# Block differences of w_out one place sooner each on VectorE, and one add ahead of the maxima of batch 3

## Chip, cores and metric

The kernel runs on one core of a Trainium2 chip. The metric is device time in microseconds (us), the median of three runs. The engines are TensorE (PE, with PEld for its weight loads), VectorE (DVE), ScalarE (ACT), GpSimd (POOL) and SyncE (SP, which here only issues transfers).

## What is computed

For each of 8 batches and 8 heads, 512 rows `x` and 32 rows `state` of width 64 read one another by attention (scale 1/8, softmax), and the result of 544 rows by 512 columns per batch goes through two dense layers with a leaky ReLU between them:

```
scores  = scale * x @ state^T          xread = softmax(scores)  @ state     # 512 rows
scores2 = scale * state @ x^T          sread = softmax(scores2) @ x         # 32 rows
x = concat([xread, sread], rows), heads side by side                        # (8*544) x 512
h = x @ w_in ; g = max(0.01*h, h)      # w_in 512 x 2048
out = g @ w_out                        # w_out 2048 x 512, fp32 out
```

## The kernel before

**Per batch.** `a_scores` puts both score matrices of a batch into one PSUM tile `sc`. The first softmax is taken over blocks of 32: `a_max` (L266), `a_diff` (a spread by 32x32 transposes, L274, and a subtraction, L280), `a_exp` (ACT, L284), `a_recip` (L289 sum, L293, L296, L298 spread), `a_probs` (L302, tile `aT`). The second softmax goes along rows: `a_max2` (L331, "the second maxima", tile `mcol`), `a_exp2` (ACT, L337, once for each half g), `a_probs2` (L345, L347, two of L355). `a_m` multiplies the states into w_in (L407, tile `M`, evicted by L421 or L1113), so that the first layer `ff1` is 16 steps s of two 512-column matmuls (L428) with a leaky ReLU on ACT (L433, tile `hT`). `a_sread` (L380) makes the 32 state rows. While batch b runs its 16 steps, the softmax of batch b+1 (`nxt`) is done between the steps.

**The second layer.** Batch 0 and half of batch 1 multiply `hT` by w_out directly (`piece`, L456; `y_store`, L466, copies a finished row block out and stores it). The rest uses a 2x2 block scheme with seven block products instead of eight: w_out is cut into blocks of 1024 rows by 256 columns, and four differences of these blocks are made once, by `tw_sum` (L495), in bf16, each in two halves of 128x1024 on DVE or four quarters of 128x512 on POOL:

- `tw[1]`: block (0,1) minus block (0,0), on POOL
- `tw[2]`: block (1,1) minus `tw[1]`, on DVE
- `tw[3]`: block (1,1) minus block (0,1), on DVE
- `tw[4]`: block (1,0) minus `tw[2]`, on DVE

Their consumers are the products: n=5 takes `tw[1]`, n=6 `tw[2]`, n=7 `tw[3]`, n=4 `tw[4]` (`w_of`). The other half of batch 1 is `two_product` (L602), done between the steps of batch 2 in the order n = 1, 2, 6, 5, 3, 7, 4 at s = 2, 3, 5, 6, 8, 9, 11. Its hT-side sums are `two_sum` (L586, tiles `Sr`); products 1, 6 and 5 are copied to `rkept` by ACT (L607), products 2, 7 and 3 are added to a kept one by DVE (L612, tile `ysb`), product 4 is copied by ACT (L609). Below these are called product 1, product 2 and so on, and the three adds of L612 add 2, add 3 and add 7. From batch 2 on `product` and `s_sum` (L551, L516) do the same for whole batches.

**Order.** The order of the instructions on each engine is written out by hand: the program's order is the order of each engine's queue, and each engine takes its own in order. At batch 2 the order at the two steps that the change touches is:

```
s == 1: a_scores(nxt) ... a_max(nxt) ... a_diff(nxt); a_max2(nxt); two_sum(q1, 3, 0, 8, nc.vector)
s == 3: two_product(q1, 2)                       # with add 2 on DVE
s == 4: a_exp(nxt) ...; tw_sum(4, ...) on DVE
```

**Other places that the steps touch.** Before batch 1, the x rows of batch 1 are cast in two halves on DVE (L898), transposed on PE (L918, tile `pxt`) and copied (L921). `state_cast` (L209) scales a group of states: for batches 2 and 3 on DVE, for batches 4 to 7 on POOL at batch 2's s = 8 (tile `stb`), after which SP issues the transposes `st_t` (L214) and, for batch 4, `xT` (L234). `cast_all` (L132) is POOL's cast of a whole batch of x, loaded by SP (L99, tile `xl`) into `xb`.

Of the kernel before, what the change touches and what calls it, by code (L numbers as in the profile page):

```python
# [27 lines left out]
def kernel(  # L28
# [9 lines left out]
    nc = tc.nc  # L38
# [290 lines left out]
    def a_max2(a):  # L329
        a.m2 = att.tile([P, 2], FP32, name="mcol", tag="mcol")  # L330
        nc.vector.tensor_reduce(out=a.m2[:], in_=a.sc[:], axis=AX.X, op=ALU.max, negate=True)  # L331
# [118 lines left out]
    def piece(b, hT, i, jq, bank=None, copy=SCA, js=range(4)):  # L450
        if jq == 0 and js[0] == 0:
            y = ys[b, i] = Y()
            y.py = psum.tile([P, DM], FP32, name="py", tag="py")[:] if bank is None else bank
        y = ys[b, i]
        for j in [4 * jq + v for v in js]:
            nc.tensor.matmul(  # L456
                y.py, lhsT=hT[:, j, P * i:P * (i + 1)], rhs=w_out_bf[:, j, :],
                start=(j == 0), stop=(j == 15),
            )
        if jq == 3 and copy is not None:  # L460
            y_store(b, i, copy)
# [8 lines left out]
    HJ = 8  # L470
# [12 lines left out]
    def w_block(r, c, j0, j1):  # L483
        return w_out_bf[:, HJ * r + j0:HJ * r + j1, HN * c:HN * (c + 1)]

    def tw_sum(n, j0, j1, eng):
        u, at = j0 // 4, slice(j0 % 4, j0 % 4 + j1 - j0)
        in0, in1 = {
            1: lambda: (w_block(0, 1, j0, j1), w_block(0, 0, j0, j1)),
            2: lambda: (w_block(1, 1, j0, j1), tw[1][u][:, at]),  # L490
            3: lambda: (w_block(1, 1, j0, j1), w_block(0, 1, j0, j1)),
            4: lambda: (w_block(1, 0, j0, j1), tw[2][u][:, at]),
        }[n]()
        with nc.allow_low_precision(reason="operands of bf16 products"):
            eng.tensor_tensor(out=tw[n][u][:, at], in0=in0, in1=in1, op=ALU.subtract)  # L495
# [431 lines left out]
    a_shift(a1)  # L927
    a_max2(a1)
    tw_open()
    for j in range(0, HJ, 2):  # L930
        tw_sum(1, j, j + 2, nc.gpsimd)
    for i in (0, 1):
        piece(0, h0, i, 1)
# [21 lines left out]
    for v in range(2):  # L955
        for i in (2, 3):
            piece(0, h0, i, 3, copy=None, js=range(2 * v, 2 * v + 2))
    for i in (2, 3):
        y_store(0, i, VEC)
    cast_all(3)  # L960
# [6 lines left out]
    for s in range(16):  # L967
        ff1(a1, h1, s)
        if s % 2:
            pb, hT, i, jq = fill[s // 2]  # L970
            piece(pb, hT, i, jq)
        if s in (1, 15):
            for u in range(2):
                tw_sum(2 if s == 1 else 3, 4 * u, 4 * (u + 1), nc.vector)
        if s == 3:
            a_scores(a2)
            m_evict(a2, 0, a_m(a2, 0, "big"), SCA)
            a_shift(a2)
            a_max2(a2)
        elif s == 7:  # L980
            a_exp(a2)
            a_open(att_of[3], 3)
            a_xt_dma(att_of[3])
        elif s in (9, 11):
            a_exp2(a2, s // 2 - 4)
            if s == 9:
                a_recip(a2)
                a_probs(a2)
            else:
                a_probs2(a2)  # L990
        elif s == 13:
            a_probs2(a1)
            a_a2t_pair(0)
            pm = [a_m(a2, 1, "big"), a_m(a2, 2, "sc")]
            m_evict(a2, 1, pm[0], VEC)
            m_evict(a2, 2, pm[1], SCA)
# [3 lines left out]
    for b in range(2, B):  # L1000
        hT = hpool.tile([P, 16, S], BF16, name="hT", tag="hT")
        hTs[b] = hT
        a = att_of[b]
        nxt = att_of[b + 1] if b + 1 < B else None
        if b == 2:
            q1 = two_open(h1, 2 * P, ("S0", "S1"), "py")
            two_keep(q1, "S2")
            fill = {i: [lambda i=i: piece(1, h1, i, 3)] for i in range(2)}
            for s, n in zip((2, 3, 5, 6, 8, 9, 11), (1, 2, 6, 5, 3, 7, 4)):
                fill[s] = [lambda n=n: two_product(q1, n)]  # L1010
            fill[11].append(lambda: nc.sync.dma_start(pair_rows(1, 1), q1.y[:]))
        else:
            order = (2, 6, 5, 7, 3, 4)
            fill = {
                s: [lambda n=order[s // 2], v=s % 2: product(b - 1, n, v)] for s in range(12)
            }
            for i, n in enumerate(order):
                if n not in (2, 7):
                    fill[2 * i + 1].append(lambda n=n: after(b - 1, n))
        fill[12 if b < 6 else 13] = [lambda: product(b, 1, 0)]  # L1020
        fill[14] = [lambda: product(b, 1, 1, 0, 4)]
        fill[15] = [lambda: product(b, 1, 1, 4, 8), lambda: after(b, 1)]
        for s in range(16):
            ff1(a, hT, s)
            if s == 0:
                if b == 2:
                    load_x(4, nc.sync)
                if b + 2 < B:
                    open_xb(b + 2)
                if b == 7:  # L1030
                    a_a2t_pair(6)
                elif b != 6:
                    a_a2t(a)
                for n in (1, 2):
                    if b > 2:
                        s_sum(b - 1, n, 4, 8, nc.vector)
                    else:
                        two_sum(q1, n, 0, 8, nc.vector)
            elif s == 1:
                if nxt is not None:  # L1040
                    a_scores(nxt)
                m_evict(a, 3, a_m(a, 3, "big"), SCA)
                if nxt is not None:
                    a_max(nxt)
                if b > 2:
                    for j in range(0, HJ, 2):
                        s_sum(b - 1, 4, j, j + 2, nc.gpsimd)
                else:
                    for j in (0, 4):
                        two_sum(q1, 4, j, j + 4, nc.gpsimd)  # L1050
                if b + 2 < B:
                    cast_all(b + 2)
            elif s == 4:
                if b == 2:
                    load_state(1)
                    a_sread(a0)
            elif s == 7:
                if b == 2:
                    a_sread(a1)
            elif s == 13:  # L1060
                if b < 6:
                    a_sread(a)
            elif s == 8:
                if b == 2:
                    state_cast(1, nc.gpsimd)
                    state_t(1)
            elif s == 10:
                if b == 7:
                    a_sread(att_of[6])
            elif s == 12:  # L1070
                if b == 7:
                    a_sread(a)
                for n in (1, 2):
                    s_sum(b, n, 0, 4, nc.vector)
                for j in (0, 4):
                    s_sum(b, 3, j, j + 4, nc.vector)
            if nxt is not None:
                if s == 4:
                    a_exp(nxt)
                elif s in (6, 7):  # L1080
                    a_exp2(nxt, s - 6)
                    if s == 7:
                        a_recip(nxt)
            if b == 2 and s == 4:
                for u in range(2):
                    tw_sum(4, 4 * u, 4 * (u + 1), nc.vector)
            if s == 9 and b + 2 < B:
                a_open(att_of[b + 2], b + 2)
                a_xt_dma(att_of[b + 2])
                if b + 3 < B:  # L1090
                    load_x(b + 3, nc.sync)
            for f in fill.get(s, ()):
                f()
            if s == 1:
                if b > 2:
                    after(b - 1, 2)
                if nxt is not None:
                    a_diff(nxt)
                    a_max2(nxt)
                if b == 2:  # L1100
                    two_sum(q1, 3, 0, 8, nc.vector)
            elif s == (8 if b == 2 else 7):
                if b > 2:
                    after(b - 1, 7)
                if nxt is not None:
                    a_probs(nxt)
                    a_probs2(nxt)
            elif s == 10 and nxt is not None:
                pm2 = a_m(nxt, 2, "phpy")
                pm0 = a_m(nxt, 0, "big")  # L1110
                pm1 = a_m(nxt, 1, "sc")
                for g, copy in enumerate((SCA, VEC)):
                    copy(nxt.M[:, g, 2 * DM:3 * DM], pm2[g][:])  # L1113
                m_evict(nxt, 0, pm0, VEC)
                m_evict(nxt, 1, pm1, SCA)
# [4 lines left out]
    b = B - 1  # L1120
# [21 lines left out]
    for n in (1, 2, 6, 5, 7, 3, 4):  # L1142
        two_product(q, n)
        if n in (3, 4):
            u = n - 3
# [43 lines left out]
```

## Time and profile before

| what | us |
|---|---|
| median of 3 runs | 206.49 (206.26 to 206.52) |
| profiled execution, its own time | 206.81 |
| its span (first to last instruction) | 205.0 |
| PE busy in the span | 198.6 (97%) |
| DVE busy | 150.9 (74%) |
| ACT busy | 142.2 (69%) |
| POOL busy | 62.3 (30%) |

The granted TensorE clock is 1.0. In the rows below the first number is the start in us from the span's beginning, the second the time until the last of the row's instructions ended; "x2" is two of them in a row; the bracket at the end is the idle time of the engine before the row and what ended it. Differences between starts are used where instructions overlap their neighbour's end, as matmuls do.

### The profile page before, as it was taken

What the parts mean: (1) busy time and instruction counts of PE and PEld (TensorE: products, weight loads), DVE (VectorE), ACT (ScalarE), POOL (GpSimd) and SP (SyncE); (2) the same over time, 40 slices, a digit from 0 to 9 for tenths busy, and PEclk for the clock granted to TensorE, in tenths of its full rate; (3) what the DMA queues carried; (4) which work ended last, traced back from release to release, by engine and by line L of the source; (5) the groups of instructions that cost most, each with busy time, mean ns of one, the idle gap of its engine ahead of it and who ended that gap; (6) DMA issues with size and microseconds to landing.
All of it is one profiled execution on the core that took longest, in us unless ns stands there. A gap on an engine that the chain in (4) does not pass through costs nothing.

```text
span 205.0 us, 4489 instructions
## 1 busy us (share of the span) xinstructions
PE 198.6 (97%) x1832; PEld 129.9 (63%) x1832; DVE 150.9 (74%) x222; ACT 142.2 (69%) x274; POOL 62.3 (30%) x67
## 2 busy tenths in 40 slices
PE   7999999999999899999999999999999999999993
PEld 2743444344465567766776677676767677788882
DVE  2765897799999999979997998699879402823512
ACT  3579767688989687867787779686958655846220
POOL 8914640030244076006700580054005400540000
PEclk9999999999999999999999999999999999999999
DMA  5999999685693796945093505220026202210115
GB/s 188 220 207 298 255 259 143 162 289 102 136 302 76 95 224 192 218 173 157 4 258 152 155 3 104 104 105 0 0 105 166 39 3 102 102 54 0 56 36 169
DMA packets 38741, 27.75 MB, mean 135 GB/s; under 512 B 24384, under 2 KB 35776, under 8 KB 38720
## 3 DMA queue, kind: packets, MB, share of 16 engines
q1 hardware_dynamic: 33552, 20.78, 39.2%
q0 software_dynamic: 4832, 6.29, 15.0%
q10 hardware_dynamic: 336, 0.39, 0.8%
q8 instruction: 14, 0.23, 0.5%
q14 instruction: 7, 0.06, 0.1%
HBM read 17.30 MB, written 8.91 MB: 128 GB/s over the span
## 4 chain that ended last, share of the span: by engine, by line
PE 71%; DVE 13%; DMA 8%; POOL 3%; issue 1%; ACT 1%; ACTq 1%; POOLq 0%
PE ph L428 19%; PE ppx L551 17%; PE ppb L551 15%; DMA x<-in_x_dram 7%; PE ppr L602 3%; PE ph L439 3%; PE pyw L456 3%; PE py L456 3%; PE ppw L551 3%; PE pm L407 3%; DVE tw L495 2%; POOL w_in_bf L145 2%; PE psr L380 1%; DVE sh L274 1%; PE sc L256 1%
## 5 line engine op out<-in xcount | busy, mean ns | idle before, releaser
L433 ACT ACTIVATE hT<-ph 128x512 bf16<-128x512 f32 x112 | 66.3, 602 | 26.6 <-PE ph L428 25.7
L428 PE MATMUL ph<-aT,M 128*128 128x512 bf16 x224 | 65.3, 379 | 0.0
L516 POOL TENSOR_TENSOR S<-hT,S 128x512 bf16<-128x512 bf16 x24 | 31.7, 1340 | 78.6 <-DVE S L516 61.5
L551 PEld LDWEIGHTS <-S 128*128 128x128 bf16 x384 | 37.6, 98 | 12.9
L551 PEld LDWEIGHTS <-hT 128*128 128x128 bf16 x288 | 27.7, 98 | 11.9 <-issue 1.9
L516 DVE TENSOR_TENSOR S<-hT 128x1024 bf16<-128x1024 bf16 x24 | 25.4, 1082 | 4.4 <-ACT hT L433 4.4
L428 PEld LDWEIGHTS <-M 128*128 128x128 bf16 x224 | 20.8, 98 | 9.3 <-issue 3.6
L551 PE MATMUL ppx<-tw,S 128*128 128x256 bf16 x160 | 20.7, 273 | 0.0
L456 PEld LDWEIGHTS <-hT 128*128 128x128 bf16 x96 | 9.0, 97 | 11.5 <-issue 1.3
L456 PE MATMUL py<-w_out_bf,hT 128*128 128x512 bf16 x64 | 16.0, 379 | 0.0
L132 POOL CAST xb<-xl 128x2048 bf16<-128x2048 f32 x5 | 9.5, 1895 | 18.1 <-DMA xl<-in_x_dram 15.2
L642 DVE TENSOR_TENSOR ysb<-ppb,s 128x512 f32<-128x512 f32 x12 | 8.3, 688 | 7.6 <-PE ppb L551 7.6
L421 ACT CAST M<-pm 128x1024 bf16<-128x1024 f32 x13 | 13.2, 1014 | 0.6 <-PE pm L407 0.6
L551 PE MATMUL ppb<-w_out_bf,hT 128*128 128x256 bf16 x96 | 12.5, 273 | 0.0
L551 PE MATMUL ppb<-tw,S 128*128 128x256 bf16 x96 | 12.4, 273 | 0.0
L551 PE MATMUL ppb<-w_out_bf,S 128*128 128x256 bf16 x96 | 12.3, 273 | 0.0
L551 PE MATMUL ppx<-w_out_bf,hT 128*128 128x256 bf16 x80 | 11.2, 273 | 0.0
L337 ACT ACTIVATE e<-sc,mcol 128x512 bf16<-128x512 f32 x16 | 11.1, 696 | 0.0
L289 DVE TRANSPOSE_TENSOR_REDUCE r<-e 128x32 f32<-128x1024 bf16 x7 | 8.7, 1243 | 2.4 <-ACT e L284 2.4
L551 PE MATMUL ppx<-tw,hT 128*128 128x256 bf16 x80 | 10.4, 273 | 0.0
L331 DVE TENSOR_REDUCE mcol<-sc 128x2 f32<-128x1024 f32 x8 | 9.7, 1215 | 0.0
L443 ACT ACTIVATE hs<-ph 128x256 bf16<-128x256 f32 x16 | 6.0, 387 | 5.0 <-PE ph L439 4.6
(135 smaller groups left out, 304.3 us busy)
## 6 DMA issues: line engine op xcount, KB each, us to landing
out_dram<-ysb SPq DMA_DIRECT2D x11, 512.0 KB, 2.7
xl<-in_x_dram SPq DMA_DIRECT2D x5, 1024.0 KB, 6.7
out_dram<-ysb SPq DMA_DIRECT2D x9, 256.0 KB, 5.1
w_in_bf<-in_moe_w_in_dram POOLq DMA_DIRECT2D x4, 512.0 KB, 9.2
xf<-in_x_dram SPq DMA_DIRECT2D x4, 256.0 KB, 3.9
w_out_bf<-in_moe_w_out_dram POOLq DMA_DIRECT2D x4, 256.0 KB, 13.8
x<-in_x_dram POOLq DMA_DIRECT2D x2, 512.0 KB, 14.2
w_out_bf<-in_moe_w_out_dram POOLq DMA_DIRECT2D x2, 512.0 KB, 15.5
```

The costliest lines, as they stand in the source:

```text
L132: nc.gpsimd.tensor_copy(xt[b][:].rearrange("p t h d -> p h t d"), xl[b][:].rearrange("p h (t d) -> p h t d", t=NT),)
L289: nc.vector.tensor_reduce(out=r1[:], in_=e1[:].rearrange("p (c j) -> p c j", j=NS), axis=AX.X, op=ALU.add, apply_transpose=True,)
L331: nc.vector.tensor_reduce(out=a.m2[:], in_=a.sc[:], axis=AX.X, op=ALU.max, negate=True)
L337: nc.scalar.activation(out=a.e2[:, g], in_=a.sc[:, g, :], func=AF.Exp, bias=a.m2[:, g:g + 1], accum_out=a.r2[:, g:g + 1],)
L407: nc.tensor.matmul(at[v][NS * r:NS * (r + 1)], lhsT=st_of(a, g, k), rhs=w_in_bf[D * g:D * (g + 1), k, DM * c:DM * (c + 1)], start=True, st ...
L421: copy(a.M[:, :, cols], pm[:])
L428: nc.tensor.matmul(ph[:], lhsT=a.M[:, g, P * j:P * (j + 1)], rhs=a.aT[:, g, :], start=(g == 0), stop=(g == 1),)
L433: nc.scalar.activation(out=hT[:, j, :], in_=ph[:], func=AF.Prelu, scale=1 / SCALE, alpha=0.01)
L456: nc.tensor.matmul(y.py, lhsT=hT[:, j, P * i:P * (i + 1)], rhs=w_out_bf[:, j, :], start=(j == 0), stop=(j == 15),)
L516: eng.tensor_tensor(out=part(n), in0=in0, in1=in1, op=op)
L551: nc.tensor.matmul(q[bank][v], lhsT=lhsT, rhs=w_of(n, j), start=q["open", bank] and j == 0, stop=j == 7, skip_group_check=True,)
L642: nc.vector.tensor_tensor(out=to, in0=of, in1=in1, op=ALU.add)
```

## The change

The reorder of POOL's four quarters of `tw[1]` puts blocks 4 to 7 ahead of blocks 0 to 3. Each DVE pair of `tw_sum` moves one place up: `tw[2]` from batch 1's s = 1 to behind the last pieces of batch 0, `tw[3]` from batch 1's s = 15 to its s = 1, `tw[4]` from batch 2's s = 4 to batch 1's s = 15. At batch 2, the second maxima and the third `two_sum` move from s = 1 to s = 3, behind `two_product(q1, 2)` and so behind add 2. No instruction is added or removed; the order on PE, ACT and SP stays as it was.

```diff
@@ before batch 1 @@
-    for j in range(0, HJ, 2):
+    for j in (4, 6, 0, 2):
         tw_sum(1, j, j + 2, nc.gpsimd)
...
             piece(0, h0, i, 3, copy=None, js=range(2 * v, 2 * v + 2))
+    for j in (0, 4):
+        tw_sum(2, j, j + 4, nc.vector)
     for i in (2, 3):
         y_store(0, i, VEC)
@@ batch 1 @@
         if s in (1, 15):
             for u in range(2):
-                tw_sum(2 if s == 1 else 3, 4 * u, 4 * (u + 1), nc.vector)
+                tw_sum(3 if s == 1 else 4, 4 * u, 4 * (u + 1), nc.vector)
@@ batches 2 to 7 @@
-            if b == 2 and s == 4:
-                for u in range(2):
-                    tw_sum(4, 4 * u, 4 * (u + 1), nc.vector)
...
                 if nxt is not None:
                     a_diff(nxt)
-                    a_max2(nxt)
-                if b == 2:
-                    two_sum(q1, 3, 0, 8, nc.vector)
+                    if b > 2:
+                        a_max2(nxt)
+            elif s == 3 and b == 2:
+                a_max2(nxt)
+                two_sum(q1, 3, 0, 8, nc.vector)
```

## The prediction

> **What bounds the kernel now.** I read the page's chain of waits first, then TensorE's (PE's) timeline around every place where the chain leaves PE, then the timelines of the engines that it goes to.
>
> ```profile
> PE 71%; DVE 13%; DMA 8%; POOL 3%; issue 1%; ACT 1%; ACTq 1%; POOLq 0%
> ```
>
> The end is set by PE, except for 13% of the span on VectorE (DVE). So a change on DVE is worth what PE's gaps in that part are worth, and no more. PE's timeline shows the gaps (start, time, engine, line; in brackets idle time and its releaser):
>
> ```profile
> 23.03 0.61 PE L918 MATMUL pxt<-ident,xb 128*128 128x128 bf16 x8
> 23.88 0.62 PE L918 MATMUL pxt<-ident,xb 128*128 128x128 bf16 x8 [0.24 <-DVE stf L902]
> 24.34 0.59 PE L456 MATMUL pyw<-w_out_bf,hT 128*128 128x512 bf16 x2
> ...
> 57.04 1.04 PE L602 MATMUL ppr<-w_out_bf,hT 128*128 128x256 bf16 x8
> ...
> 60.12 0.59 PE L428 MATMUL ph<-aT,M 128*128 128x512 bf16 x2
> 60.85 1.05 PE L602 MATMUL ppr<-tw,Sr 128*128 128x256 bf16 x8
> ...
> 62.63 0.59 PE L428 MATMUL ph<-aT,M 128*128 128x512 bf16 x2
> 63.06 1.04 PE L602 MATMUL ppr<-w_out_bf,Sr 128*128 128x256 bf16 x8
> ...
> 65.24 0.59 PE L428 MATMUL ph<-aT,M 128*128 128x512 bf16 x2
> 65.77 0.39 PE L407 MATMUL pm<-w_in_bf,st_t 64*32 64x512 bf16 x1
> 66.75 0.84 PE L407 MATMUL pm<-w_in_bf,st_t 64*32 64x512 bf16 x23 [0.60 <-DVE ysb L612]
> 67.53 0.60 PE L428 MATMUL ph<-aT,M 128*128 128x512 bf16 x2
> 68.61 1.03 PE L602 MATMUL ppr<-tw,hT 128*128 128x256 bf16 x8 [0.48 <-DVE ysb L612]
> ```
>
> By starts: a transpose group takes 0.46 (23.88 to 24.34), but the first one held PE 0.85, a gap of 0.39. A pair of L428 takes 0.43 (62.63 to 63.06), so product 5 at 60.85 is 0.30 late, the matmuls for M are about 0.95 late (65.77 to 66.75 for one of them), and product 4 at 68.61 is 0.65 late. Together 2.29 us: the most that this change can return. DVE ends all of these waits; its rows:
>
> ```profile
> 21.28 0.68 DVE L898 CAST xb<-x 128x1024 bf16<-128x1024 f32 x1
> 22.22 1.60 DVE L898 CAST xb<-x 128x1024 bf16<-128x1024 f32 x1 [0.26 <-DMA x<-in_x_dram]
> ...
> 36.86 1.29 DVE L466 COPY ysb<-pyw 128x512 f32<-128x512 f32 x2 [1.31 <-PE pyw L456]
> ...
> 40.69 1.25 DVE L266 TRANSPOSE_TENSOR_REDUCE mrow<-sc 128x32 f32<-128x1024 f32 x1 [0.41 <-PE sc L256]
> ...
> 52.42 1.29 DVE L495 TENSOR_TENSOR tw<-w_out_bf 128x1024 bf16<-128x1024 bf16 x2
> ...
> 58.65 1.22 DVE L331 TENSOR_REDUCE mcol<-sc 128x2 f32<-128x1024 f32 x1
> 59.78 0.68 DVE L586 TENSOR_TENSOR Sr<-hT 128x1024 bf16<-128x1024 bf16 x1
> 60.38 0.42 DVE L612 TENSOR_TENSOR ysb<-ppr,rkept 128x256 f32<-128x256 f32 x1
> 60.71 2.04 DVE L495 TENSOR_TENSOR tw<-w_out_bf,tw 128x1024 bf16<-128x1024 bf16 x1
> ...
> 63.28 1.23 DVE L289 TRANSPOSE_TENSOR_REDUCE r<-e 128x32 f32<-128x1024 bf16 x1
> ...
> 65.15 1.25 DVE L298 STREAM_TRANSPOSE qb<-qh 128x1024 bf16<-128x1024 bf16 x1
> 66.32 0.39 DVE L612 TENSOR_TENSOR ysb<-ppr,rkept 128x256 f32<-128x256 f32 x1
> 66.63 0.67 DVE L302 TENSOR_TENSOR aT<-e,qb 128x1024 bf16<-128x1024 bf16 x1
> ...
> 67.61 0.62 DVE L355 TENSOR_SCALAR a<-e,qc 128x512 bf16<-128x512 bf16 x2
> 68.14 0.42 DVE L612 TENSOR_TENSOR ysb<-ppr,rkept 128x256 f32<-128x256 f32 x1
> ```
>
> From 40.69 on DVE is full. Two of its rows are far too long: the second L898 cast (1.60 beside 0.68) and the first tw difference at 60.71 (2.04, where the pair at 52.42 took 1.29 together). GpSimd's (POOL's) rows lie across both:
>
> ```profile
> 22.12 2.71 POOL L495 TENSOR_TENSOR tw<-w_out_bf 128x512 bf16<-128x512 bf16 x2 [0.78 <-DVE xb L898]
> 25.90 2.27 POOL L495 TENSOR_TENSOR tw<-w_out_bf 128x512 bf16<-128x512 bf16 x2 [1.06 <-DMA w_out_bf<-in_moe_w_out_dram]
> ...
> 60.31 1.90 POOL L132 CAST xb<-xl 128x2048 bf16<-128x2048 f32 x1 [2.86 <-PE ppr L602]
> 65.08 1.50 POOL L209 TENSOR_SCALAR stb<-stf 128x512 bf16<-128x512 f32 x1 [2.87 <-DMA stf<-in_state_dram]
> ```
>
> So while POOL works, some DVE instructions stand: the difference issued at 60.71 ended at 62.75, 0.54 behind POOL's 62.21, and with 0.68 of its own it began about 62.07, 0.14 before POOL's recorded end.
>
> **POOL's order.** The quarters of blocks 4 to 7 wait for w_out until 25.90 in either order, and now stand first. Nothing of POOL lies on the cast at 22.22 any more: it ends at 22.90 instead of 23.82, the second transposes follow the first at 23.49, and PE is 0.39 earlier from there. POOL ends at about 30.4 (25.90 + 4 x 1.13) instead of 28.17. The first reader of tw[1] is DVE's new place at 35.16 (36.86 - 1.31 - 0.39), so 4.7 us of other work cover that; past them, a delay would hold DVE's queue us for us.
>
> **tw[2] behind batch 0.** DVE idles 1.31 ahead of 36.86, waiting for PE's pieces. The pair costs 1.29 and fills this hole; were it later, the copies, batch 0's second probabilities and tw[3] stand behind it, and only the 0.41 idle before 40.69 absorbs it. I price it at nothing. tw[3] takes tw[2]'s place and tw[4] takes the place at 52.42, pair for pair. So everything from 40.69 to 58.65 moves by the 0.39 that PE gained, and no more.
>
> **Batch 2.** What stood on DVE from 58.65 was maxima, Sr 3, add 2, two tw differences, L289. Now it is add 2, maxima, Sr 3, L289. The steps from start to start are 0.33 (60.38 to 60.71), 1.13 (58.65 to 59.78) and 0.60 (59.78 to 60.38). Add 2 starts at 58.65 - 0.39 = 58.26; product 2 ended at 57.04 + 1.04 = 58.08, now 57.69, so it waits for nothing. Maxima 58.59, Sr 3 59.72, L289 60.32: 2.96 before 63.28, of which 0.39 is the early gain and 2.57 the tw pair with its stall. ScalarE (ACT) doesn't forbid it:
>
> ```profile
> 59.58 1.06 ACT L284 ACTIVATE e<-sh 128x1024 bf16<-128x1024 f32 x1
> ...
> 64.53 1.07 ACT L433 ACTIVATE hT<-ph 128x512 bf16<-128x512 f32 x2
> ```
>
> L289's input was there at 60.64, now 60.25. With add 2 gone by 58.7, product 5 loses its 0.30.
>
> What is late next: POOL's cast asks for its turn at 60.31 - 0.39 = 59.92, if its transfer moves with the rest: SP issues it behind the transposes of batch 0's second probabilities, which DVE writes. Sr 3 was first by 0.20, so POOL waits about 0.35 and DVE nothing. Then L298 at 62.19 (+1.87), add 3 at 63.36, held to about 63.45 by product 3 (63.06 + 1.04 less 0.69), L302 at 63.76, L355 at 64.74. POOL's state cast, whose transfers follow in the same queue, moves to 64.69 and holds until 66.19 - 0.14 = 66.05. L355 falls inside. Its kind (one input, no PSUM) was not seen beside POOL; it costs between nothing and a stall to 66.05. I take the stall, by the nearest row: the L898 cast has one input too and was held. Then add 7 starts at 66.05 + 0.53 = 66.58 and product 4 at 67.05 (+0.47, as 68.14 to 68.61): 1.56 earlier than 68.61.
>
> The Trainium skill, SBUF — State Buffer, section "Who interferes with whom", says that a DVE instruction with two SBUF inputs, or a copy, cast or tensor_scalar in a two-port mode, takes a port pair that POOL needs too, for the whole instruction, and that whichever starts first keeps the other out. That rule speaks against this change, since it moves a two-input sum to within 0.2 us of a POOL cast; by it the sum would be rival 2's where POOL is first, and by the rows alone 1.56.
>
> Behind product 4 PE has no gap of this size until batch 3, where the transposed x of batch 4 could be late:
>
> ```profile
> 67.90 3.03 SPq L234 DMA_TRANSPOSE xT<-xb  x1
> ...
> xT<-xb SPq DMA_TRANSPOSE x1, 5.4
> ...
> 75.25 0.41 PE L256 MATMUL sc<-xT,st_t 64*32 64x512 bf16 x8
> ```
>
> It landed at 73.30; its issue follows POOL's state cast, so now 72.9, and PE asks at 75.25 - 1.56 = 73.69. That holds. The sum is **-1.56 us**: 0.39 early and 1.17 at batch 2. Against the profiled execution's own 206.81 that is 205.25; the median of the runs is 0.32 lower, 206.49, and gives 204.9.
>
> **Rivals.** (1) The state cast comes later than L355's second half, or doesn't hold it. Then add 7 starts at 65.27 and PE is the later one. ACT's queue of activations was back to back until 65.60, so PE's pair at 65.24 gains only about 0.44 (to 64.80); the next pair follows 2.29 - 0.95 = 1.34 later, product 4 0.43 after it, 66.57: -2.04, 204.4. For it: the two are 0.05 us apart. Against it: the cast lasts 1.50 and need only touch the second half.
>
> (2) POOL's cast at 59.92 gets in ahead of Sr 3. Sr 3 starts at 61.81 - 0.14 = 61.67, L289 at 62.27, add 3 at 65.31, and L302 at 65.62 meets the state cast, until 66.05. Product 4 then starts 1.98 later (66.63 to 68.61), 68.03: -0.58, 205.9. Without the second meeting it is 67.60: -1.01, 205.5. For it: a lead of 0.20 against a transfer. Against it: both follow from the same DVE work.
>
> (3) Rival 2, and no early gain, because PE's second transposes wait for something other than the cast (the row names a memset beside it). -0.58 + 0.39 = -0.19: no change that can be told.
>
> (4) Slower. Add 2 now stands ahead of the maxima, so whatever it waits for holds them, Sr 3 and L289. It writes a y tile, and stores of y tiles are under way:
>
> ```profile
> 57.44 1.00 SPq L467 DMA_DIRECT2D out_dram<-ysb  x2
> ...
> out_dram<-ysb SPq DMA_DIRECT2D x1, 256.0 KB, 4.7
> ```
>
> If its buffer were free only when the first of these lands, 62.14, now 61.75, L289 would start 2.06 later, 63.81, 0.53 behind 63.28: about +0.5, 207.0. It decides from an add later than 61.22. Against it: before, the add ran at 60.38 right behind Sr 3, with no idle time.
>
> **How the numbers follow.** Forecast 0.47, rival 1 0.18, rival 2 0.22, rival 3 0.08, rival 4 0.05. A measurement of this kernel can tell 0.2%, 0.41 us, from no change. Faster takes the forecast and rivals 1 and 2, 0.87; same is rival 3, 0.08; slower rival 4, 0.05. The range takes in rivals 1 and 2 with some 0.1 to 0.2 of scatter (the runs span 0.26): 204.2 to 206.0.
>
> **What would show it.** In the changed profile: the second L898 cast near 0.7; PE's second transposes at about 23.5; the tw[2] pair ending by 36.5 with no idle left ahead of L466; add 2 at about 58.3 and L289 at about 60.3; no tw difference beyond 54; L355 long, beside POOL's state cast; product 4 at about 67.05. It is wrong if Sr 3 shows the 2 us (rival 2), if L355 is short (rival 1), if idle time stands ahead of add 2 (rival 4), or if PE waits in batch 3 where it did not before.

## The result and the profile after

The changed kernel takes 204.70 us (median of 6, 204.28 to 204.96) beside 206.51 us (median of 6, 206.26 to 206.78) for the kernel before: 1.81 us less, ratio 0.9908 with a 95% interval of 0.9895 to 0.9922. Here and below, the ratios leave out single executions in a slower state of the chip, and the medians take all. The profiled execution took 204.43 us with a span of 202.7, 2.3 less than the span before. Of this, 0.53 is not the change's: PE's first transposes, which lie ahead of all edits, start at 22.50 instead of 23.03. From there on everything is read by steps.

The page's chain of waits, and PE's timeline of the changed kernel at the places shown of before:

```profile
PE 87%; DMA 6%; ACT 2%; POOL 2%; ACTq 1%; issue 1%; POOLq 0%
```

```profile
22.50 1.23 PE L918 MATMUL pxt<-ident,xb 128*128 128x128 bf16 x16
23.56 0.59 PE L456 MATMUL pyw<-w_out_bf,hT 128*128 128x512 bf16 x2
...
59.78 1.04 PE L602 MATMUL ppr<-tw,Sr 128*128 128x256 bf16 x8
...
61.55 0.60 PE L428 MATMUL ph<-aT,M 128*128 128x512 bf16 x2
62.23 1.03 PE L602 MATMUL ppr<-w_out_bf,Sr 128*128 128x256 bf16 x8
...
64.93 0.84 PE L407 MATMUL pm<-w_in_bf,st_t 64*32 64x512 bf16 x24
...
66.15 1.04 PE L602 MATMUL ppr<-tw,hT 128*128 128x256 bf16 x8
```

DVE is out of the chain (13% before) and no bracket with idle time is left at these places. The 16 transposes run together, the 24 matmuls for M too, and product 4 follows the pair ahead of it at once. Product 4 stands 43.65 behind the first transposes (22.50 to 66.15); before it was 45.58 (23.03 to 68.61). That is 1.93 us, near the 1.81 between the medians. One place got worse: product 3, at 62.23, stands 0.68 behind the pair ahead of it, where 0.43 is usual. DVE's, POOL's and ACT's timelines:

```profile
22.36 0.69 DVE L898 CAST xb<-x 128x1024 bf16<-128x1024 f32 x1 [0.93 <-DMA x<-in_x_dram]
...
34.69 1.29 DVE L495 TENSOR_TENSOR tw<-w_out_bf,tw 128x1024 bf16<-128x1024 bf16 x2
36.09 1.29 DVE L466 COPY ysb<-pyw 128x512 f32<-128x512 f32 x2
...
38.22 1.29 DVE L495 TENSOR_TENSOR tw<-w_out_bf 128x1024 bf16<-128x1024 bf16 x2
...
51.64 1.28 DVE L495 TENSOR_TENSOR tw<-w_out_bf,tw 128x1024 bf16<-128x1024 bf16 x2
...
57.87 0.41 DVE L612 TENSOR_TENSOR ysb<-ppr,rkept 128x256 f32<-128x256 f32 x1
58.20 1.21 DVE L331 TENSOR_REDUCE mcol<-sc 128x2 f32<-128x1024 f32 x1
59.33 0.68 DVE L586 TENSOR_TENSOR Sr<-hT 128x1024 bf16<-128x1024 bf16 x1
59.93 1.24 DVE L289 TRANSPOSE_TENSOR_REDUCE r<-e 128x32 f32<-128x1024 bf16 x1
61.20 0.59 DVE L293 TENSOR_SCALAR r<-r 128x32 f32<-128x32 f32 x1
...
63.39 0.41 DVE L612 TENSOR_TENSOR ysb<-ppr,rkept 128x256 f32<-128x256 f32 x1
63.71 0.68 DVE L302 TENSOR_TENSOR aT<-e,qb 128x1024 bf16<-128x1024 bf16 x1
64.31 0.16 DVE L345 TENSOR_SCALAR r<-r 128x2 f32<-128x2 f32 x1
...
64.71 0.68 DVE L355 TENSOR_SCALAR a<-e,qc 128x512 bf16<-128x512 bf16 x2
65.31 0.41 DVE L612 TENSOR_TENSOR ysb<-ppr,rkept 128x256 f32<-128x256 f32 x1
```

```profile
26.14 4.49 POOL L495 TENSOR_TENSOR tw<-w_out_bf 128x512 bf16<-128x512 bf16 x4 [4.57 <-DMA w_out_bf<-in_moe_w_out_dram]
...
59.53 2.23 POOL L132 CAST xb<-xl 128x2048 bf16<-128x2048 f32 x1 [2.86 <-PE ppr L602]
64.37 1.50 POOL L209 TENSOR_SCALAR stb<-stf 128x512 bf16<-128x512 f32 x1 [2.61 <-DMA stf<-in_state_dram]
```

```profile
61.12 0.70 ACT L337 ACTIVATE e<-sc,mcol 128x512 bf16<-128x512 f32 x1
...
61.79 0.39 ACT L607 COPY rkept<-ppr 128x256 f32<-128x256 f32 x1
```

The second L898 cast is 0.69 long; the tw[2] pair fills the idle stretch ahead of L466, and the pairs for tw[3] and tw[4] take 1.29 and 1.28 in their new places; the order at batch 2 is add 2, maxima, Sr 3, L289, and from add 2 to L289 it is 2.06. POOL's cast is 2.23 long instead of 1.90: it waited for Sr 3. The copy of product 5 ends on ACT at 62.18, and product 3, which goes into the same bank, starts at 62.23: that is the new wait.

### The profile page after: what moved, and what is told of

The parts are those of the page before. It is cut to its first block, busy times and chain, and to the rows that moved or that the text cites. A ratio compares the mean times of both kernels' runs of the same rounds, so it can differ in the third digit from the quotient of the medians.

```text
span 202.7 us, 4489 instructions
## 1 busy us (share of the span) xinstructions
PE 197.6 (98%) x1832; PEld 129.4 (64%) x1832; DVE 149.1 (74%) x222; ACT 141.9 (70%) x274; POOL 62.2 (31%) x67
## 4 chain that ended last, share of the span: by engine, by line
PE 87%; DMA 6%; ACT 2%; POOL 2%; ACTq 1%; issue 1%; POOLq 0%
PE ph L428 24%; PE ppx L551 17%; PE ppb L551 15%; PE py L456 7%; DMA w_in_bf<-in_moe_w_in_dram 5%; PE ppr L602 5%; PE pm L407 4%; PE pyw L456 4%; PE ph L439 3%; PE ppw L551 3%; PE sc L256 2%; PE psr L380 1%; PE ph L850 1%; PE php L850 1%; DMA out_dram<-ysb 1%; POOL w_in_bf L145 1%
## 5 line engine op out<-in xcount | busy, mean ns | idle before, releaser
L433 ACT ACTIVATE hT<-ph 128x512 bf16<-128x512 f32 x112 | 66.3, 603 | 26.4 <-PE ph L428 25.5
L428 PE MATMUL ph<-aT,M 128*128 128x512 bf16 x224 | 65.3, 379 | 0.0
L516 POOL TENSOR_TENSOR S<-hT,S 128x512 bf16<-128x512 bf16 x24 | 31.6, 1337 | 75.6 <-DVE S L516 58.5
L516 DVE TENSOR_TENSOR S<-hT 128x1024 bf16<-128x1024 bf16 x24 | 25.3, 1077 | 4.7 <-ACT hT L433 4.6
L428 PEld LDWEIGHTS <-M 128*128 128x128 bf16 x224 | 20.9, 98 | 9.3 <-issue 3.6
L456 PEld LDWEIGHTS <-hT 128*128 128x128 bf16 x96 | 9.0, 98 | 11.4 <-issue 1.3
L456 PE MATMUL py<-w_out_bf,hT 128*128 128x512 bf16 x64 | 16.0, 379 | 0.0
L289 DVE TRANSPOSE_TENSOR_REDUCE r<-e 128x32 f32<-128x1024 bf16 x7 | 8.7, 1244 | 2.5 <-ACT e L284 2.5
L331 DVE TENSOR_REDUCE mcol<-sc 128x2 f32<-128x1024 f32 x8 | 9.7, 1214 | 0.0
```

Of the source, the lines that this page charges most:

```text
L289: nc.vector.tensor_reduce(out=r1[:], in_=e1[:].rearrange("p (c j) -> p c j", j=NS), axis=AX.X, op=ALU.add, apply_transpose=True,)
L428: nc.tensor.matmul(ph[:], lhsT=a.M[:, g, P * j:P * (j + 1)], rhs=a.aT[:, g, :], start=(g == 0), stop=(g == 1),)
L433: nc.scalar.activation(out=hT[:, j, :], in_=ph[:], func=AF.Prelu, scale=1 / SCALE, alpha=0.01)
L456: nc.tensor.matmul(y.py, lhsT=hT[:, j, P * i:P * (i + 1)], rhs=w_out_bf[:, j, :], start=(j == 0), stop=(j == 15),)
L516: eng.tensor_tensor(out=part(n), in0=in0, in1=in1, op=op)
```

## The experiments

Each compares with runs of the kernel before beside it on the same chip; the changed kernel was run again in two of the three groups. Since the start of the program varies by about 1 us from one profile to another, the profiles are compared by steps between PE's starts: from the first transposes to the pieces behind them (L918 to L456), from batch 1's first L428 pair to product 3, from product 3 to product 4.

| kernel | ratio, 95% interval | median us (before beside it) | L918 to L456 | to product 3 | to product 4 |
|---|---|---|---|---|---|
| before | 1 | 206.51 | 1.31 | 26.40 | 5.55 |
| changed | 0.9908 (0.9895 to 0.9922) | 204.70 (206.51) | 1.06 | 26.35 | 3.92 |
| changed, again | 0.9907 (0.9889 to 0.9926) | 204.61 (206.57) | 1.06 | 26.35 | 4.32 |
| POOL's order alone | 0.9979 (0.9966 to 0.9993) | 205.94 (206.57) | 1.09 | 26.42 | 5.55 |
| changed, POOL's old order | 0.9920 (0.9908 to 0.9932) | 205.03 (206.57) | 1.96 | 26.36 | 4.32 |
| changed, add 2 where it was | 0.9891 (0.9878 to 0.9904) | 204.37 (206.57) | 1.19 | 26.41 | 4.31 |
| POOL's order and add 2, no tw moves | 1.0006 (0.9986 to 1.0027) | 206.97 (206.82) | 0.89 | 26.35 | 5.93 |
| product 5's copy on DVE | 0.9910 (0.9888 to 0.9931) | 204.87 (206.82) | 0.90 | 26.09 | 3.92 |
| state cast early | 0.9904 (0.9885 to 0.9924) | 204.77 (206.82) | 0.89 | 26.34 | 3.92 |
| changed, third time | 0.9904 (0.9879 to 0.9929) | 204.64 (206.64) | 0.90 | 26.35 | 3.92 |
| load of batch 4 early | 0.9895 (0.9870 to 0.9920) | 204.47 (206.64) | 0.90 | 26.35 | 3.92 |
| both of the two edits | 0.9882 (0.9857 to 0.9908) | 204.30 (206.64) | 1.22 | 26.10 | 4.09 |

The first column is not read alone: where it is 0.89 or 0.90, the step behind it, from the pieces to batch 1's first pair, is 12.47 instead of 12.32, so that the two together are 13.36 or 13.37 there and 13.38 in the changed kernel's first profile (13.63 before).

### The yardstick

The changed kernel itself, with no edit.

> The changed kernel once more, as the yardstick for the others of this group. Every theory expects what was measured, -1.8 us against the kernel before.

It gave the same ratio, but not the same profile: its DVE and POOL timelines, and PE at product 4, are

```profile
64.05 0.57 DVE L345 TENSOR_SCALAR r<-r 128x2 f32<-128x2 f32 x1
...
64.86 1.03 DVE L355 TENSOR_SCALAR a<-e,qc 128x512 bf16<-128x512 bf16 x2
```

```profile
63.96 1.52 POOL L209 TENSOR_SCALAR stb<-stf 128x512 bf16<-128x512 f32 x1 [2.46 <-DMA stf<-in_state_dram]
```

```profile
66.28 1.03 PE L602 MATMUL ppr<-tw,hT 128*128 128x256 bf16 x8 [0.23 <-DVE ysb L612]
```

Here the state cast asked 0.09 before L345, not 0.06 after it, and it held L345 by 0.41 and the two L355 by 0.41 together. Product 4 then waits: 4.32 instead of 3.92. So the second collision of the prediction does occur, in one of the changed kernel's three profiles, and costs PE 0.40 there. The time doesn't show it: this profile's first transposes started 0.27 sooner, and its span is 202.7 too.

### POOL's order, alone and taken out

```diff
-    for j in range(0, HJ, 2):     # before; "alone" makes this edit in the kernel before,
+    for j in (4, 6, 0, 2):        # "taken out" undoes it in the changed kernel
         tw_sum(1, j, j + 2, nc.gpsimd)
```

> The kernel before with POOL's quarters of tw[1] in the new order and nothing else. Theory A (the early stall of the cast L898 behind POOL's quarter is on PE's path, everything behind it moves by it, and the three gaps at batch 2 stay): the second cast takes 0.7 instead of 1.6, PE's second transposes follow the first ones, -0.25 us (the step from the first transposes to the matmuls behind them was 1.31 before and 1.06 after). Rival B (DVE's full stretch from batch 1 on is not reached earlier, or another wait takes its place): 0.0.

> The changed kernel with POOL's quarters of tw[1] back in the old order. Theory A: the cast L898 is held again, PE starts batch 0's pieces 0.25 us later, and all else stays: -1.55 us against the kernel before, 0.25 behind the changed one. Rival B (the early part is worth nothing by itself): -1.8.

Alone it gave ratio 0.9979, by the ratio -0.43 us (-0.14 to -0.70), with both steps at batch 2 as long as before (26.42 and 5.55): theory A. Taken out, 0.27 us of the gain goes (0.9920 beside 0.9907; the intervals overlap). What it costs depends on when PE arrives; with the old order, PE's and DVE's timelines:

```profile
23.79 0.62 PE L918 MATMUL pxt<-ident,xb 128*128 128x128 bf16 x8 [0.89 <-DVE stf L902]
```

```profile
22.24 1.49 DVE L898 CAST xb<-x 128x1024 bf16<-128x1024 f32 x1 [0.56 <-DMA x<-in_x_dram]
```

In this profile PE came early and waited 0.89 for the held cast (in the profile before, 0.24). The row names L902, a small memset that stands right behind the cast on DVE; where the cast is short, the transposes no longer wait, although the memset is still there.

### Add 2 back where it was

```diff
                 if nxt is not None:
                     a_diff(nxt)
-                    if b > 2:
-                        a_max2(nxt)
-            elif s == 3 and b == 2:
-                a_max2(nxt)
-                two_sum(q1, 3, 0, 8, nc.vector)
+                    a_max2(nxt)
+                if b == 2:
+                    two_sum(q1, 3, 0, 8, nc.vector)
```

> The changed kernel with the second maxima and Sr 3 back at s = 1, ahead of add 2; the tw pairs and POOL's order stay in their new places. Theory A: add 2 starts at about 59.6 instead of 57.9, so product 5 is late by 0.2 to 0.3 us again, but product 3 waits anyway for ACT's copy of product 5, whose time is set by ACT's own queue; nothing is lost, -1.8 us. Rival B (the add's place is worth the gap that it closes): 0.25 to 0.30 less gain, -1.5.

0.9891: nothing lost, as theory A had it. PE's timeline shows why:

```profile
59.94 1.05 PE L602 MATMUL ppr<-tw,Sr 128*128 128x256 bf16 x8
...
61.72 0.59 PE L428 MATMUL ph<-aT,M 128*128 128x512 bf16 x2
62.16 1.04 PE L602 MATMUL ppr<-w_out_bf,Sr 128*128 128x256 bf16 x8
```

Product 5 comes late again, and product 3 no longer waits (0.44 behind its pair): the 0.30 is paid at product 5 instead of 0.25 at product 3, and the step to product 3 is 26.41 instead of 26.35. This part of the change is worth nothing that can be measured.

### Everything but the tw moves

The edits are POOL's order and the order at s = 3, in the kernel before; `tw_sum(4)` stays at s = 4, `tw_sum(2)` and `tw_sum(3)` in batch 1.

> The kernel before with POOL's new order and with the new order at batch 2 (add 2, second maxima, Sr 3 at s = 3), but with all tw pairs at their old places, so tw[4] still stands between Sr 3 and L289. Theory A (the gain at batch 2 is the tw pair with its stall leaving DVE's queue): add 2 early closes product 5's gap of 0.30, but add 3 and add 7 come when they came, PE waits there by so much longer, and nothing is left beyond POOL's order: about -0.4 us against the kernel before, as with POOL's order alone. Rival B (the add's place is worth its own gap): 0.3 more, -0.7.

No gain at all (1.0006): closing product 5's gap did not help, as theory A said, and even the 0.4 that theory A left for POOL's order is not seen. DVE's and POOL's timelines:

```profile
60.73 2.98 DVE L495 TENSOR_TENSOR tw<-w_out_bf,tw 128x1024 bf16<-128x1024 bf16 x2
```

```profile
60.51 2.05 POOL L132 CAST xb<-xl 128x2048 bf16<-128x2048 f32 x1 [3.04 <-DMA xl<-in_x_dram]
```

Sr 3 now stands later and keeps POOL's cast waiting, so the cast ends later, and the tw pair behind it takes 2.98 instead of 2.65; from product 3 to product 4 it is 5.93. So of the 1.9 us, the part at batch 2 comes from the tw[4] pair leaving that place, its stall included; the new place of add 2 by itself makes the stall longer.

### The new bound: ACT's copy of product 5, and the state cast

```diff
-        if n in (1, 6, 5):
+        if n == 5 and q.r0:                       # batch 1 only
+            VEC(q.kept[n], q.bank[w])             # DVE, queued between L289 and L293
+        elif n in (1, 6, 5):
             SCA(q.kept[n], q.bank[w])
```

```diff
@@ batch 1, s == 3 @@
+            load_state(1)                         # was at batch 2, s == 4
@@ batch 2, s == 1, behind Sr 4 @@
+                    state_cast(1, nc.gpsimd)      # was at s == 8
```

> The changed kernel with the copy of product 5 into its kept place done by DVE, right behind L289, instead of ACT. Theory A (product 3 now waits for ACT, which is the new bound there): the 0.25 us ahead of product 3 goes, L293 starts when POOL's cast is about to end and loses its stall, so DVE's queue ends no later; 0.0 to 0.25 better than the changed kernel, -1.9 to -2.2 against the kernel before, the smaller figure where product 4 then waits for add 7. Rival B (DVE is still the bound): its 0.4 goes onto add 7, 0.3 worse than the changed kernel, -1.6.

> The changed kernel with the loads of the second state group issued in batch 1 and POOL's state cast put right behind its Sr 4 quarters, ahead of the cast of batch 4, so that it lies beside DVE work that reads PSUM. Theory A (the state cast holds L345 and L355 by 0.4 us each, and that is what product 4 waits for): L345 0.16, L355 0.62 for two, product 4 without a wait, 0.2 better than the changed kernel, -2.1 against the kernel before. Rival B (product 4's time is set by ACT and PE): no difference, -1.9.

Both do in the profile what theory A says. With the copy on DVE, product 3 comes 0.43 behind its pair and the step to it is 26.09; DVE pays nothing for the copy, since L293 stood for POOL's cast there anyway. PE's and DVE's timelines:

```profile
61.54 0.38 PE L433 MATMUL ph<-aT,M 128*128 128x512 bf16 x1
61.97 1.04 PE L607 MATMUL ppr<-w_out_bf,Sr 128*128 128x256 bf16 x8
```

```profile
61.09 0.39 DVE L612 COPY rkept<-ppr 128x256 f32<-128x256 f32 x1
61.40 0.40 DVE L298 TENSOR_SCALAR r<-r 128x32 f32<-128x32 f32 x1
```

(Lines are shifted by the edit: L433 is the ff1 pair, L607 the product, L298 the old L293. The code shown leaves out that the edit also splits `a_recip`, so that L289 comes ahead of product 5's copy and L293 behind it.) With the state cast early, L345 and L355 run free and product 4 comes 3.92 behind product 3, as it does in two of the changed kernel's three profiles. In time neither can be told from the changed kernel (0.9910 and 0.9904 beside 0.9907 and 0.9904). Both together:

> The changed kernel with both of the last two edits: product 5's copy on DVE behind L289, and the state loads and POOL's state cast moved ahead. Theory A (what is left at batch 2 is ACT's copy ahead of product 3, 0.25, and the state cast beside L345 and L355, 0 or 0.40): from the first ff1 pair of batch 1 to product 3 26.09 instead of 26.35, from there to product 4 3.92 in every profile; 0.25 to 0.65 better than the changed kernel beside it, about -2.3 us against the kernel before. Rival B (ACT's activations set product 4 anyway): product 4 comes when it came, -1.9.

> The changed kernel once more, as the yardstick beside the others of this group: -1.8 to -2.0 us against the kernel before by every theory; 3.92 or 4.32 from product 3 to product 4, as the state cast falls.

204.30 us, ratio 0.9882, 0.34 us below the changed kernel beside it, within the forecast by theory A's lower end, but the intervals overlap. It is the lowest median of the group; that it beats the changed kernel isn't shown by the time. In its profile product 3 is 0.25 earlier, as meant, while product 4 lost 0.17 to add 7, against the 3.92 expected in every profile: POOL's cast came 0.93 behind Sr 3 in this profile, not 0.20, and held the old L293 to 0.79.

### POOL first at the port

```diff
             a_probs2(a1)
+            load_x(4, nc.sync)                    # was at batch 2, s == 0
             a_a2t_pair(0)
```

> The changed kernel with batch 4's x loaded ahead of the transposes of batch 0's and 1's second probabilities, so that POOL's cast waits only for its buffer (free after batch 0's sread, about 1.2 us ahead of where it asked) and is first at the port when Sr 3 comes. Theory A (DVE has slack now): Sr 3 stands for 0.7, L289 is later by as much, L293 is no longer held; add 3 0.3 later, still ahead of PE's matmuls for M; product 4 where it was, -1.8 us against the kernel before. Rival B (the prediction's rival 2: POOL first costs what Sr 3 stands): product 4 0.6 to 0.9 later, -1.0 to -1.2.

Ratio 0.9895: no loss, theory A. DVE's and POOL's timelines:

```profile
59.89 1.37 DVE L586 TENSOR_TENSOR Sr<-hT 128x1024 bf16<-128x1024 bf16 x1
61.19 1.23 DVE L289 TRANSPOSE_TENSOR_REDUCE r<-e 128x32 f32<-128x1024 bf16 x1
62.45 0.18 DVE L293 TENSOR_SCALAR r<-r 128x32 f32<-128x32 f32 x1
```

```profile
58.83 1.89 POOL L132 CAST xb<-xl 128x2048 bf16<-128x2048 f32 x1 [1.59 <-PE psr L380]
62.78 1.50 POOL L209 TENSOR_SCALAR stb<-stf 128x512 bf16<-128x512 f32 x1 [2.06 <-DMA stf<-in_state_dram]
```

Sr 3 stands 0.69, L293 no longer does, and product 4 is 3.92 behind product 3. But POOL's cast was 1.06 ahead of Sr 3 here, so only its last part fell on it, and the state cast came sooner too, beside L298, so that L345 and L355 ran free (0.16 and 0.62). The prediction's rival 2 had the cast just ahead of Sr 3, which would then start 1.95 later; that case was not run. An estimate from the profile after: DVE runs without a pause from L289 to add 7, L293 would give back 0.41, and add 7 ended 0.43 ahead of product 4's start, so that of 1.95 about 1.1 would reach product 4.

### What stands while POOL works

The edit repeats `cast_all(4)` and `state_cast(1, nc.gpsimd)` three times each, writing the same values.

> The changed kernel with POOL's cast of batch 4 done three times over, and its state cast three times over, to see which DVE instructions stand while POOL works. Theory A (each instruction with two SBUF inputs, and each cast or tensor_scalar, stands until POOL's running instruction ends): L293 about 0.6, L302 or the two L355 1 to 2 us long, the sums of L516 beside the state casts about 1.5 each, L298, L266, L331 and the adds from PSUM as long as ever; the time 2 to 4 us more than the changed kernel. Rival B (a tensor_scalar is let in part of the way, as it seemed beside the state cast): L355 and L345 longer by 0.4 each at most, the sums by as much.

One run, 211.01 us, some 6 us above the changed kernel where 2 to 4 were expected. In its profile PE waits 2.96 for the later x of batch 4 and 1.23 for add 7; the rest stays open. POOL's and DVE's timelines, and the shortest, middle and longest of POOL's three casts of each kind in ns:

```profile
60.62 6.37 POOL L132 CAST xb<-xl 128x2048 bf16<-128x2048 f32 x3 [3.11 <-DMA xl<-in_x_dram]
66.97 5.03 POOL L209 TENSOR_SCALAR stb<-stf 128x512 bf16<-128x512 f32 x3
```

```profile
64.55 0.68 DVE L302 TENSOR_TENSOR aT<-e,qb 128x1024 bf16<-128x1024 bf16 x1
65.15 1.86 DVE L345 TENSOR_SCALAR r<-r 128x2 f32<-128x2 f32 x1
...
67.24 0.75 DVE L355 TENSOR_SCALAR a<-e,qc 128x512 bf16<-128x512 bf16 x2
...
69.97 0.68 DVE L516 TENSOR_TENSOR S<-hT 128x1024 bf16<-128x1024 bf16 x1
70.68 0.98 DVE L516 TENSOR_TENSOR S<-S,hT 128x1024 bf16<-128x1024 bf16 x1
```

```profile
L132 POOL CAST xb<-xl x3: 1897/1982/2364, 60.6 to 64.6; 128x2048 bf16<-128x2048 f32 x3
L209 POOL TENSOR_SCALAR stb<-stf x3: 1490/1501/1872, 67.0 to 70.1; 128x512 bf16<-128x512 f32 x3
```

Each theory has half. The x cast holds an instruction to its end: L345, of 128x2 elements, took 1.86 instead of 0.16. L302 (0.68) came just between the second and the third cast, and the third one waited for it: 2.36 instead of 1.90. The state cast lets DVE in before its end: two L355 cost 0.13 more than 0.62, and the second L516 sum 0.29 more than 0.69. The first L516 sum says nothing on this, since it came in ahead of the third state cast, which took 1.87 instead of 1.50 for it.

## Why the prediction was right, point by point

- **PE's gaps as the ceiling: right.** 2.29 us was the most to be had; 1.93 came in the profile. No idle time of PE opened in batch 3.
- **POOL's order: right in kind, its size depends on the start.** Forecast 0.39; the step gave 0.25 (the x half landed at 22.36, and the cast ended behind PE's first transposes), POOL's order alone measured 0.43 (0.14 to 0.70).
- **tw[2] in the hole ahead of L466, tw[3] and tw[4] at no cost: right.** The pair took 1.29 and L466 followed without idle time; the pairs in the two other places took 1.29 and 1.28.
- **The order at batch 2: right to 0.01.** From add 2, L331, Sr 3 and L289 follow after 0.33, 1.46 and 2.06, which is what the sum used; POOL's cast was second by 0.20 and waited 0.33.
- **The second collision: mis-sized.** The step "L355 falls inside ... I take the stall" put 1.31 on add 7. It measured 0.06 in the profile after and 0.82 on DVE in the next one (L345 and L355 together), of which PE saw 0.40. The state cast let DVE in before its end; the held row that I took for the nearest stood beside two-input sums of POOL. So the case that came is rival 1 (-2.04 forecast, -1.93 by steps, -1.81 by medians), and the forecast of -1.56 was 0.25 short. By the prediction's own sign (L355 long) its main case did not come; the time lies in its range because the range took in rival 1. Of the 1.93, batch 2 gave 1.68, where the main case had 1.17 and rival 1 had 1.65.
- **Missed: L293.** This small tensor_scalar stood 0.41 for POOL's cast. It cost PE nothing, since add 3 ended 1.1 us ahead of M's matmuls and add 7 0.43 ahead of product 4.
- **Missed: product 3 waits for ACT's copy of product 5.** Closing product 5's 0.30 opened 0.25 here. The prediction reckoned with ACT's full queue only at the pair of 65.24; it already sets product 3, a few steps sooner.
- **Rival 2 (POOL first) did not come, and its price is open.** It put 0.98 to 1.03 more on product 4 than the cases with Sr 3 first, for a Sr 3 that starts 1.95 later. A hold of 0.69 cost nothing, since L293 gave back 0.41 and add 7 had 0.43 to spare; by the same rows 1.95 would cost about 1.1 (an estimate), near the rival's price. Rivals 3 and 4 didn't show: the second transposes no longer wait, and no idle time stands ahead of add 2.

## What to carry to other kernels

Count the gain of a faster queue in the gaps of the engine that sets the end, and then ask of each closed gap who is next: here 0.25 of the 0.30 us of one gap only moved from DVE to ACT, and one of the edits could be left out at no loss for that reason. Keep DVE's two-input, cast and tensor_scalar instructions on SBUF out of the stretches where POOL casts or sums, or put POOL's work beside DVE instructions that read PSUM, which here kept their usual time. Compare profiles by steps between landmarks, since the start alone varied by 1.1 us here.

## What the runs showed of the hardware

A POOL instruction doesn't hold DVE by its length alone. The 128x2048 cast of 1.90 us kept even a tensor_scalar of 128x2 waiting to its end (1.86 instead of 0.16). The state cast, a POOL tensor_scalar of 1.50 us, held single DVE tensor_scalars by 0.04 to 0.43 in the changed kernel's three profiles. The two L355 of the profile after and of the yardstick (shortest, mean of the two and longer one, in ns):

```profile
L355 DVE TENSOR_SCALAR a<-e,qc x2: 343/380/418, 64.7 to 65.0; 128x512 bf16<-128x512 bf16 x2
L355 DVE TENSOR_SCALAR a<-e,qc x2: 334/556/779, 64.9 to 65.6; 128x512 bf16<-128x512 bf16 x2
```

Where L355 was the first to meet the state cast, it took 0.42 instead of 0.35 and ended 0.75 ahead of the cast's end; where L345 had met it first, the first L355 took 0.78 and ended 0.15 behind it. By an estimate (its end less its usual time) the first DVE instruction got in 0.40 after the state cast's start in the one case and 0.50 in the other. The Trainium skill, SBUF — State Buffer, section "Who interferes with whom", has the shared port pair held for the whole instruction; the cast agrees with that (1.70 us of waiting), the state cast doesn't, by the first L355 of the profile after. Why it lets DVE in was not tried.
